# Half of the first product's tiles from seven products of quarters in blocks 2 to 5

## The chip, the cores and the metric

One Trainium2 chip, one core. The metric is the device time of one execution in microseconds (us); the kernel before has a median of 204.72 us in 3 runs.

## The reference, cut to what matters

Two stages: a recurrent attention with decay per head, and a two-layer network over its output with a leaky ramp whose slope differs by column.

```python
# q, k, v: (4, 8, 768, 64); w_in: (512, 2048); w_out: (2048, 512); alpha: (2048,)
for t in range(S):
    state = gamma * state + outer(k[:, :, t], v[:, :, t])
    y[:, :, t] = scale * q[:, :, t] @ state
x = y.transpose(0, 2, 1, 3).reshape(3072, 512)
h = x @ w_in
g = maximum(h, 0) + alpha * minimum(h, 0)
out = g @ w_out
```

## The kernel before, in words

**Blocks and units.** The 3072 tokens are 6 blocks of 512; a block is two units of 256. A unit's attention is done in chunks: GpSimd (or VectorE, early) rescales k and q by powers of the decay into `kdq` (`rescale`, L149) and casts v (`cast_v`, L162); a DMA transpose on SP's queue (`turn_dma`, L170) makes `kq`; TensorE makes state sums (`sum_mm`, L204) and scores (`score_mm`, L258); VectorE masks the scores (`masks`, L277) and adds up the state (`state`, L227: ss on VectorE, tf and tg on GpSimd or ScalarE); TensorE makes the output (`out_mm`, L289), and ScalarE evicts it, transposed, into `xT` (`take_y`, L325).

**First product** (`ffn1`, L364): gT = gate(w_inT xT) of one block, 16 tiles of 128 columns of w_in by 512 tokens. A tile is four matmuls of 512 columns into one PSUM bank. ScalarE writes hm = relu(-h) to SBUF (L389); VectorE adds (1-alpha) * hm to h from PSUM and writes f16 `gt` (L391). The tiles go in pairs f, f+8. VectorE then makes sums and differences of quarters of `gt` (`g_sums`, L351, into a tile `gs`): two of the four behind the first product, two in the second.

**Second product** (`ffn2_seven`, L433), blocks 1 to 5: out = g w_out by seven products of quarters (16 matmuls of 256 columns each) in place of eight, as `gs` and `wsum` (`w_sums`, L341) hold the sums that this takes. Their order: `gt` times w_out (1), again into `oy` (2), `gs` 1 (3), `gs` 0 (4), `gs` 2 (5), `gt` (6), `gs` 3 (7). ox and oy are PSUM banks 0 and 1. ScalarE keeps partial results (`kept`, tile `cu`), VectorE adds them to others from PSUM (`plus`, tile `os`).

**Order.** The schedule is written out by hand: each engine runs its instructions in the order in which the program emits them, and waits on semaphores for the others. `ffn1` and `ffn2_seven` are generators that yield after each matmul, and `tick(gen, m)` (L540) takes m matmuls' worth. In the loop over blocks (L703) the body emits the first product of block n with GpSimd's rescales of the units of block n+1 (the first of them held back behind the last `g_sums` by `behind`, L100), then the second product of block n with the attention of block n+1 between its pieces: after half of product 1 the state sums and scores of the first unit, after product 3 its output and the second unit's scores, after product 5 the second unit's output. Blocks 0 and 1 have a prologue of their own, written out above the loop.

**Buffers.** A tile of a tag waits until the reader of the tile that held its buffer is done. All 8 PSUM banks are addressed by number: `ps(bank, ...)`.

Of the kernel before, what the change touches and what calls it, by code (L numbers as in the profile page):

```python
# [9 lines left out]
FP = mybir.dt.float32  # L10
F16 = mybir.dt.float16
# [2 lines left out]
RELU = mybir.ActivationFunctionType.Relu  # L14
MULT = mybir.AluOpType.mult
ADD = mybir.AluOpType.add
EQUAL = mybir.AluOpType.is_equal
NOT_LESS = mybir.AluOpType.is_ge

# [2 lines left out]
def kernel(  # L22
# [117 lines left out]
    def unit(u):  # L140
        if u not in prepped:
            prepped[u] = (
                sbp.tile([128, 2, 2, H, D], F16, tag="kdq", bufs=4, name=f"kdq{u}"),
                sbp.tile([128, 4 * NP, 128], F16, tag="kq", bufs=4, name=f"kq{u}"),
                sbp.tile([128, H, 2, D], F16, tag="vx", bufs=4, name=f"vx{u}"),
            )
        return prepped[u]

# [127 lines left out]

    def masks(u, hh, parts=(0, 1)):  # L277
        for a in parts:
            m2 = sbp.tile([128, 2, 2, 128], F16, tag=f"m2{a}{hh}", bufs=2, name=f"m2{a}{hh}")
            i = nc.vector.tensor_tensor(  # L280
                out=m2,
                in0=live[u, hh][a].rearrange("p (r a i) -> p r a i", r=2, a=2),
                in1=mask.unsqueeze(2).to_broadcast([128, 2, 2, 128]),
                op=MULT,
            )
            live[u, hh][a] = m2
        return i
# [37 lines left out]
    def take_y(u, cs):  # L325
        n, ul = divmod(u, 2)
        if n not in xT:
            xT[n] = sbp.tile([128, 2, NP, U], F16, tag="xT", bufs=2, name=f"xT{n}")
# [22 lines left out]
    def g_sums(n, i, lo, hi):  # L351

        if n not in gsums:
            gsums[n] = sbp.tile([128, 4, HF, U], F16, tag="gt", bufs=2, name=f"gs{n}")
        g = gts[n].rearrange("p (k f) (j t) -> p k f j t", k=2, j=2)
        a11, a12 = g[:, 0, lo:hi, 0, :], g[:, 1, lo:hi, 0, :]
        a21, a22 = g[:, 0, lo:hi, 1, :], g[:, 1, lo:hi, 1, :]
        s1, s2, s3, s4 = (gsums[n][:, x, lo:hi, :] for x in range(4))
        o, a, b, op = (
            (s1, a21, a22, ADD), (s2, s1, a11, SUB), (s3, a11, a21, SUB), (s4, a12, s2, SUB)  # L360
        )[i]
        return nc.vector.tensor_tensor(out=o, in0=a, in1=b, op=op)  # L362

    def ffn1(n, banks, apart=0):  # L364
# [5 lines left out]
        rest = range(apart, NFT)  # L370
        if apart == 0:
            rest = [f + x for f in range(HF) for x in (0, HF)]
        turns += [(f, 1, 0, 2) for f in rest]
        for i, (f0, nf, lo, hi) in enumerate(turns):
            hps = ps(banks[i % len(banks)], "hps").rearrange("p (f t) -> p f t", f=nf)
            for f in range(nf):
                for hp in range(4):
                    nc.tensor.matmul(  # L378
                        out=hps[:, f, :].rearrange("p (u t) -> p u t", t=U),
                        lhsT=w_in_all[:, hp, 128 * (f0 + f) : 128 * (f0 + f) + 128],  # L380
                        rhs=xT[n][:, lo:hi, hp, :],
                        start=(hp == 0),
                        stop=(hp == 3),
                    )
                    if f < nf - 1 or hp < 3:
                        yield
            hm = sbp.tile([128, TB], FP, tag="hm", bufs=3, name="hm")
# [11 lines left out]
            if n > 0 and f0 in ((HF + 3, NFT - 1) if apart == 0 else (NFT - 1,)):  # L399

                lo = 0 if apart or f0 < NFT - 1 else 4
                hi = HF if f0 == NFT - 1 else 4
                g_sums(n, 0, lo, hi)
                g_sums(n, 1, lo, hi)
            yield

    def ffn2(n, banks, parts=1):
        gt = gts.pop(n)
        opss = {}
        step = NFT // parts  # L410
        for f0 in range(0, NFT, step):
            for tq in range(4):
                if f0 == 0:
                    opss[tq] = ps(banks[tq % len(banks)], "ops")
                for ft in range(f0, f0 + step):
                    nc.tensor.matmul(  # L416
                        out=opss[tq],
                        lhsT=gt[:, ft, 128 * tq : 128 * tq + 128],
                        rhs=w_out_all[:, ft, :],
                        start=(ft == 0),  # L420
                        stop=(ft == NFT - 1),
                    )
                    if ft == NFT - 1:
                        tag = ("os", "cu")[tq % 2]
                        os_sb = sbp.tile([128, d_model], FP, tag=tag, bufs=3, name=tag)
                        nc.scalar.activation(
                            out=os_sb, in_=opss[tq], func=COPY, bias=0.0, scale=1.0
                        )
                        row = TB * n + 128 * tq
                        nc.sync.dma_start(out=out[row : row + 128, :], in_=os_sb)  # L430
                    yield

    def ffn2_seven(n, x, y, z=None):  # L433
# [41 lines left out]
                        yield  # L475

        def kept(o):
            t = sbp.tile([128, 2, HM], FP, tag="cu", bufs=3, name="cu")
            for to, i in [(t, o[0])] if o[0] is not None else zip((t[:, 0, :], t[:, 1, :]), o[1]):
                nc.scalar.activation(out=to, in_=i, func=COPY, bias=0.0, scale=1.0)  # L480
            return t

        def plus(o, t, name="os"):
            so = sbp.tile([128, 2, HM], FP, tag=name, bufs=3, name=name)
            nc.vector.tensor_tensor(out=so, in0=o[0], in1=t, op=ADD)  # L485
            return so

# [188 lines left out]
    score_mm(3, 0, (4, 5))  # L676
# [106 lines left out]
```

## Time and profile before

| what | value |
|---|---|
| median of 3 runs | 204.72 us (204.43 to 205.89) |
| the profiled execution | 206.04 us |
| its span, first to last instruction | 204.3 us |
| granted TensorE clock | 1.00 in all of it |
| first products of blocks 2 to 5 start at | 85.16, 115.12, 144.84, 174.80 us |
| their length on TensorE | 13.81 us each |
| VectorE busy in that of block 3 (115.12 to 128.93) | 12.09 us |
| VectorE busy in block 3's second product (128.93 to 144.84, 15.91 us) | 12.04 us |
| ScalarE, GpSimd busy in block 3's first product | 8.96, 5.64 us |
| second product of block 5, to the end of the span | 188.61 to 204.3 us |

The engines' names: PE is TensorE, PEld its weight loads, DVE VectorE, ACT ScalarE, POOL GpSimd, SP the queue that issues most DMAs. A row of the chain or of the timeline gives start, length, engine, line, output<-inputs, shape and how many; in brackets the idle time before it and who ended it. Busy time of TensorE counts pipelined matmuls, so the spacing of matmuls is read from the chain.

### The profile page before, as it was taken

How to read it: one execution, taken by the hardware profiler on the slowest of the kernel's cores; microseconds unless marked ns; L12 is line 12 of the kernel's file. 1: busy time of each engine (PE TensorE's matmuls, PEld its weight loads, DVE VectorE, ACT ScalarE, POOL GpSimd, SP SyncE). 2: the span in 40 equal slices, each digit the busy share in tenths (PEclk: the TensorE clock that was granted, in tenths of full speed). 3: DMA queues.
4: the chain of work that ended last, by engine and by line, in shares of the span. 5: the costliest groups of instructions: out<-in, count | busy, mean ns of one | idle time of the engine just before them, and what ended most of it. 6: DMA issues, size and time to landing. Idle time of an engine off the chain costs nothing.

```text
span 204.3 us, 5491 instructions
## 1 busy us (share of the span) xinstructions
PE 195.2 (96%) x2314; PEld 128.2 (63%) x2314; DVE 157.0 (77%) x246; ACT 101.9 (50%) x169; POOL 83.3 (41%) x96
## 2 busy tenths in 40 slices
PE   7789997999999999999999999999999999999993
PEld 2457543566574788744788644788544888545882
DVE  7794985646899999189998289996489995589841
ACT  2465665236376333477353466333476254466311
POOL 2289117480269553970065960165930250000000
PEclk9999999999999999999999999999999999999999
DMA  5998999599997799399911499910570011200004
GB/s 158 337 234 134 185 253 235 157 249 173 299 346 223 153 340 304 110 258 304 284 46 41 149 250 281 300 55 22 176 166 0 3 52 57 103 0 0 21 33 154
DMA packets 64696, 33.94 MB, mean 166 GB/s; under 512 B 18064, under 2 KB 64160, under 8 KB 64672
## 3 DMA queue, kind: packets, MB, share of 16 engines
q1 hardware_dynamic: 60272, 29.37, 50.0%
q0 software_dynamic: 4224, 4.19, 13.4%
q8 instruction: 18, 0.29, 0.6%
q10 hardware_dynamic: 176, 0.03, 0.1%
q14 instruction: 6, 0.05, 0.1%
HBM read 27.30 MB, written 6.29 MB: 164 GB/s over the span
## 4 chain that ended last, share of the span: by engine, by line
PE 73%; DMA 16%; DVE 3%; POOL 2%; SPq 2%; issue 2%; ACT 0%; POOLq 0%; DVEq 0%
PE hps L378 32%; PE ox L464 16%; PE oy L464 11%; DMA qs<-in_q_dram 6%; PE ops L416 5%; DMA wout<-in_moe_w_out_dram 4%; DMA win<-in_moe_w_in_dram 4%; DMA ks<-in_k_dram 3%; PE y L313 2%; SPq L132 2%; PE sca L268 2%; PE y L298 1%; POOL tf L241 1%; PE st L215 1%; PE oz L464 1%
## 5 line engine op out<-in xcount | busy, mean ns | idle before, releaser
L378 PE MATMUL hps<-xT,win 128*128 128x512 f16 (+1 forms) x432 | 84.5, 355 | 0.1
L391 DVE SCALAR_TENSOR_TENSOR gt<-hm,oma,hps 128x512 f16<-128x512 f32 (+1 forms) x108 | 70.8, 685 | 13.6 <-ACT hm L389 8.1
L389 ACT ACTIVATE hm<-hps 128x512 f32<-128x512 f32 x96 | 57.3, 597 | 33.6 <-PE hps L378 31.4
L378 PEld LDWEIGHTS <-win 128*128 128x128 f16 x432 | 42.0, 98 | 40.3 <-DMA win<-in_moe_w_in_dram 0.8
L464 PEld LDWEIGHTS <-gs 128*128 128x128 f16 x320 | 31.0, 98 | 3.9
L241 POOL TENSOR_TENSOR tf<-ss,tab 128x256 f32<-128x256 f32 x16 | 12.2, 765 | 35.7 <-DVE ss L240 34.7
L464 PEld LDWEIGHTS <-gt 128*128 128x128 f16 x240 | 22.8, 98 | 4.8
L152 POOL TENSOR_TENSOR kdq<-ks,tab 128x1024 f16<-128x1024 f32 (+1 forms) x10 | 17.3, 1729 | 18.8 <-issue 9.8
L480 ACT ACTIVATE cu<-ox 128x512 f32<-128x512 f32 (+1 forms) x18 | 9.5, 526 | 29.9 <-PE ox L464 29.7
L256 POOL CAST tg<-tf 64x256 f16<-64x256 f32 x29 | 14.2, 488 | 20.0 <-DVE tf L237 18.6
L485 DVE TENSOR_TENSOR os<-oy,cu 128x512 f32<-128x512 f32 x14 | 9.6, 689 | 16.2 <-PE oy L464 13.7
L152 POOL TENSOR_TENSOR kdq<-qs,tab 128x1024 f16<-128x1024 f32 (+1 forms) x13 | 20.7, 1594 | 1.9 <-DMA qs<-in_q_dram 1.9
L280 DVE TENSOR_TENSOR m<-sca,mi 128x512 f16<-128x512 f32 x24 | 16.4, 684 | 4.2 <-PE scb L268 4.2
L464 PE MATMUL ox<-wsum,gs 128*128 128x256 f16 x160 | 19.1, 273 | 0.0
L331 ACT ACTIVATE xT<-y 128x512 f16<-128x512 f32 x24 | 16.2, 741 | 5.6 <-PE y L313 5.5
L280 DVE TENSOR_TENSOR m<-scb,mi 128x512 f16<-128x512 f32 x24 | 16.3, 681 | 0.0
L416 PE MATMUL ops<-wout,gt 128*128 128x512 f16 x64 | 15.2, 380 | 0.2 <-DMA wout<-in_moe_w_out_dram 0.2
L168 POOL CAST vx<-vs 128x1024 f16<-128x1024 f32 (+1 forms) x13 | 12.5, 973 | 5.6 <-DMA vs<-in_v_dram 5.6
L362 DVE TENSOR_TENSOR gs<-gt 128x1024 f16<-128x1024 f16 (+1 forms) x14 | 12.9, 922 | 0.3
L254 ACT ACTIVATE tg<-tf 64x256 f16<-64x256 f32 x11 | 4.6, 414 | 15.6 <-POOL tf L241 10.4
L188 ACT ACTIVATE kq<-trb 128x1024 f16<-128x1024 f16 x8 | 8.2, 1024 | 6.7 <-PE trb L182 6.5
L464 PE MATMUL ox<-wout,gt 128*128 128x256 f16 x80 | 10.4, 274 | 0.0
(50 smaller groups left out, 175.1 us busy)
## 6 DMA issues: line engine op xcount, KB each, us to landing
out_dram<-os SPq DMA_DIRECT2D x21, 256.0 KB, 2.3
vs<-in_v_dram SPq DMA_DIRECT2D x10, 512.0 KB, 6.4
ks<-in_k_dram SPq DMA_DIRECT2D x8, 512.0 KB, 4.6
qs<-in_q_dram SPq DMA_DIRECT2D x8, 512.0 KB, 5.5
ks<-in_k_dram SPq DMA_DIRECT2D x8, 256.0 KB, 4.7
qs<-in_q_dram SPq DMA_DIRECT2D x8, 256.0 KB, 4.8
win<-in_moe_w_in_dram POOLq DMA_DIRECT2D x4, 512.0 KB, 8.0
wout<-in_moe_w_out_dram POOLq DMA_DIRECT2D x4, 512.0 KB, 8.5
```

The source lines that it names most:

```text
L152: return eng.tensor_tensor(out=kdq[:, t, :, h0:h1, :].rearrange("p r h d -> p h r d"), in0=staged[u]["kq"[t]][:, h0:h1, :].rearrange("p h ...
L168: eng.tensor_copy(out=o, in_=i)
L241: eng.tensor_tensor(out=t, in0=ss, in1=dec, op=MULT)
L256: nc.gpsimd.tensor_copy(out=o, in_=i)
L280: i = nc.vector.tensor_tensor(out=m2, in0=live[u, hh][a].rearrange("p (r a i) -> p r a i", r=2, a=2), in1=mask.unsqueeze(2).to_broadcast([ ...
L331: nc.scalar.activation(out=xT[n][:, ul, :, 128 * c : 128 * c + 128].rearrange("k a (p r) -> k a r p", r=2), in_=ys[c].rearrange("k (a r p) ...
L362: return nc.vector.tensor_tensor(out=o, in0=a, in1=b, op=op)
L378: nc.tensor.matmul(out=hps[:, f, :].rearrange("p (u t) -> p u t", t=U), lhsT=w_in_all[:, hp, 128 * (f0 + f) : 128 * (f0 + f) + 128], rhs=x ...
L389: nc.scalar.activation(out=hm, in_=hps, func=RELU, bias=0.0, scale=-1.0)
L391: nc.vector.scalar_tensor_tensor(out=gt[:, f0 + f, U * lo : U * hi], in0=hm[:, f, :], scalar=oma_sb[:, f0 + f : f0 + f + 1], in1=hps[:, f, :],
L416: nc.tensor.matmul(out=opss[tq], lhsT=gt[:, ft, 128 * tq : 128 * tq + 128], rhs=w_out_all[:, ft, :], start=(ft == 0), stop=(ft == NFT - 1),)
L464: nc.tensor.matmul(out=o[1][m], lhsT=lhs(f, m), rhs=rhs(f), start=(first and f == 0 and (m == 0 or o[0] is None)), stop=(f == HF - 1), ski ...
```

## The change

In the first product of blocks 2 to 5, the tiles 0 to 3 and 8 to 11 are made as two groups (g = 0, 1) of two-by-two quarters: rows are the tile halves (i = 0: tiles 2g, 2g+1; i = 1: tiles 8+2g, 9+2g), columns the two units j of the block, and the contraction is halved too. Seven products of four 256-column matmuls give the four quarters c11, c21, c12, c22 of a group. This takes sums of quarters of w_in (`wi_sums`, once, on VectorE in the prologue) and of `xT` (`x_sums`, per block, on VectorE). The other eight tiles (`one`) are made as before and lie between the groups. ScalarE keeps c1, u2 and u3, VectorE adds them to PSUM (`plus`: c11, c22, c12, in SBUF as f32), and c21 comes from PSUM. c11 and c22 are gated on GpSimd (`gate_pool`), c21 and c12 by ScalarE's relu and VectorE's gate, by quarters. To make room, `kdq`, `kq`, `vx` go from 4 to 3 buffers, `m2` and `xT` from 2 to 1; `hm` goes from 3 to 5, `cu` from 3 to 4. `ffn1` stays for blocks 0 and 1.

```diff
+    amo_sb = sbp.tile([128, 128], FP, tag="amo", name="amo")[:, 0:NFT]
+    SEV = 4
+    visum = sbp.tile([128, 4, 2, 128 * SEV], F16, tag="visum", name="visum")
...
+    def wi_sums(x):
+        a11, a12 = wi_quarter(0, 0, 0, SEV), wi_quarter(0, 1, 0, SEV)
+        a21, a22 = wi_quarter(1, 0, 0, SEV), wi_quarter(1, 1, 0, SEV)
+        s1, s2, s3, s4 = (visum[:, y] for y in range(4))
+        o, a, b, op = (
+            (s1, a21, a22, ADD), (s2, s1, a11, SUB), (s3, a11, a21, SUB), (s4, a12, s2, SUB)
+        )[x]
+        nc.vector.tensor_tensor(out=o, in0=a, in1=b, op=op)
...
+    def x_sums(n):
+        t = sbp.tile([128, 4, 2, U], F16, tag="xsum", name=f"xsum{n}")
+        xsum[n] = t
+        (b11, b21), (b12, b22) = (
+            [xT[n][:, j, 2 * k : 2 * k + 2, :] for k in range(2)] for j in range(2)
+        )
+        t1, t2, t3, t4 = (t[:, y] for y in range(4))
+        for o, a, b in ((t1, b12, b11), (t2, b22, t1), (t3, b22, b12), (t4, b21, t2)):
+            nc.vector.tensor_tensor(out=o, in0=a, in1=b, op=SUB)
...
+        def gate_pool(i, g, h, j):
+            f = HF * h + 2 * g
+            hm = sbp.tile([128, TB], FP, tag="hm", bufs=5, name="hm")
+            for x in range(2):
+                c = slice(U * x, U * x + U)
+                nc.gpsimd.tensor_scalar(
+                    out=hm[:, c],
+                    in0=i[:, c],
+                    scalar1=0.0,
+                    scalar2=amo_sb[:, f + x : f + x + 1],
+                    op0=MIN,
+                    op1=MULT,
+                )
+            nc.gpsimd.tensor_tensor(
+                out=gt[:, f : f + 2, U * j : U * j + U],
+                in0=hm.rearrange("p (f t) -> p f t", f=2),
+                in1=i.rearrange("p (f t) -> p f t", f=2),
+                op=ADD,
+            )
...
+        def product(p, g, o, first):
+            for x in range(2):
+                w = lhs(p, 2 * g + x)
+                for h in range(2):
+                    nc.tensor.matmul(
+                        out=o[:, U * x : U * x + U],
+                        lhsT=w[h],
+                        rhs=rhs[p][:, h, :],
...
+        def plus(o, t):
+            so = sbp.tile([128, TB], FP, tag="os", bufs=3, name="os")
+            nc.vector.tensor_tensor(out=so, in0=o, in1=t, op=ADD)
+            return so
...
+        yield from one(SEV, 7)
+        yield from one(HF + SEV, 2)
+        yield from one(SEV + 1, 3)
+        for g in range(2):
+            X[g] = ps((4, 6)[g], "hx")
+            yield from product(1, g, X[g], True)
+            c1[g] = kept(X[g])
+            yield
+        for g in range(2):
+            Y[g] = ps((5, 1)[g], "hy")
+            yield from product(2, g, Y[g], True)
+            c11[g] = plus(Y[g], c1[g])
+            yield
+        yield from one(HF + SEV + 1, 0)
+        for g in range(2):
+            yield from product(6, g, X[g], False)
+            u2[g] = kept(X[g])
+            gate_pool(c11[g], g, 0, 0)
+            yield
+        for g in range(2):
+            yield from product(5, g, Y[g], True)
+            yield
+        yield from one(SEV + 2, 7)
+        for g in range(2):
+            yield from product(7, g, X[g], False)
+            u3[g] = kept(X[g])
+            c22[g] = plus(Y[g], u3[g])
+            gate_pool(c22[g], g, 1, 1)
+            yield
+        yield from one(HF + SEV + 2, 2)
+        for g in range(2):
+            yield from product(4, g, X[g], False)
+            gate_by(X[g], relu(X[g]), parts(g, 1, 0))
+            yield
+        yield from one(SEV + 3, 3)
+        for g in range(2):
+            yield from product(3, g, Y[g], False)
+            c12[g] = plus(Y[g], u2[g])
+            yield
+        yield from one(HF + SEV + 3, 7)
+        for g in range(2):
+            gate_by(c12[g], relu(c12[g]), parts(g, 0, 1))
+        for lo, hi in ((SEV, HF), (0, SEV)):
+            g_sums(n, 0, lo, hi)
+            g_sums(n, 1, lo, hi)
...
+    V.tensor_scalar(out=amo_sb, in0=oma_sb, scalar1=-1.0, scalar2=None, op0=MULT)
     w_sums(0, 0, HF)
     tick(gen, 9)
     out_mm(2, (4, 5))
     tick(gen, 10)
-    tick(half, 24)
+    tick(half, 16)
+    wi_sums(0)
+    wi_sums(1)
+    tick(half, 8)
+    wi_sums(2)
     turn_pe(3, 0, 6)
     tick(half, 8)
+    wi_sums(3)
...
-            gen = ffn1(n, (7, 2, 3, 1, 0, 6, 5, 4, 7, 1, 0, 4, 5, 6, 7, 1))
+            gen = ffn1_mixed(n)
...
             out_mm(u0 + 1, (4, 5))
+            x_sums(n + 1)
```

More of the change, by code (lines that the diff above doesn't have):

```diff
@@ L16 @@
 ADD = mybir.AluOpType.add
+MIN = mybir.AluOpType.min
 EQUAL = mybir.AluOpType.is_equal
@@ new lines, with ffn1_mixed, one, relu @@
+    xsum = {}
+    def x_sums(n):
[7 more added lines that the diff above has]
+            nc.vector.tensor_tensor(out=o, in0=a, in1=b, op=SUB)
+    def ffn1_mixed(n):
+        gt = sbp.tile([128, NFT, TB], F16, tag="gt", bufs=2, name=f"gt{n}")
+        gts[n] = gt
+        b = [[xT[n][:, j, 2 * k : 2 * k + 2, :] for j in range(2)] for k in range(2)]
+        xs = [xsum[n][:, y] for y in range(4)]
+        def one(f, bank):
+            hps = ps(bank, "hps")
+            for hp in range(4):
+                nc.tensor.matmul(
+                    out=hps.rearrange("p (u t) -> p u t", t=U),
+                    lhsT=w_in_all[:, hp, 128 * f : 128 * f + 128],
+                    rhs=xT[n][:, :, hp, :],
+                    start=(hp == 0),
+                    stop=(hp == 3),
+                )
+                if hp < 3:
+                    yield
+            gate_by(hps, relu(hps), [(f, 0, 2, 0)])
+            yield
+        def relu(i):
+            hm = sbp.tile([128, TB], FP, tag="hm", bufs=5, name="hm")
+            nc.scalar.activation(out=hm, in_=i, func=RELU, bias=0.0, scale=-1.0)
+            return hm
+        def gate_by(i, hm, parts):
+            for f, lo, hi, at in parts:
+                c = slice(at, at + U * (hi - lo))
+                nc.vector.scalar_tensor_tensor(
+                    out=gt[:, f, U * lo : U * hi],
+                    in0=hm[:, c],
+                    scalar=oma_sb[:, f : f + 1],
+                    in1=i[:, c],
+                    op0=MULT,
+                    op1=ADD,
+                )
+        def gate_pool(i, g, h, j):
+            f = HF * h + 2 * g
+            hm = sbp.tile([128, TB], FP, tag="hm", bufs=5, name="hm")
+            for x in range(2):
[7 more added lines that the diff above has]
+                    op1=MULT,
+                )
+            nc.gpsimd.tensor_tensor(
[3 more added lines that the diff above has]
+                op=ADD,
+            )
+        def lhs(p, f):
+            if p in (1, 2, 4):
+                i, k = ((0, 0), (0, 1), (1, 1))[(1, 2, 4).index(p)]
+                w = wi_quarter(i, k, f, f + 1)
+            else:
+                w = visum[:, {3: 3, 5: 0, 6: 1, 7: 2}[p], :, 128 * f : 128 * f + 128]
+            return [w[:, h, :] for h in range(2)]
+        rhs = {1: b[0][0], 2: b[1][0], 3: b[1][1], 4: xs[3], 5: xs[0], 6: xs[1], 7: xs[2]}
+        def product(p, g, o, first):
+            for x in range(2):
+                w = lhs(p, 2 * g + x)
+                for h in range(2):
+                    nc.tensor.matmul(
+                        out=o[:, U * x : U * x + U],
+                        lhsT=w[h],
+                        rhs=rhs[p][:, h, :],
+                        start=(first and x == 0 and h == 0),
+                        stop=(h == 1),
+                        skip_group_check=True,
+                    )
+                    if x == 0 or h == 0:
+                        yield
+        def kept(o):
+            t = sbp.tile([128, TB], FP, tag="cu", bufs=4, name="cu")
+            nc.scalar.activation(out=t, in_=o, func=COPY, bias=0.0, scale=1.0)
+            return t
+        def plus(o, t):
+            so = sbp.tile([128, TB], FP, tag="os", bufs=3, name="os")
+            nc.vector.tensor_tensor(out=so, in0=o, in1=t, op=ADD)
+            return so
+        def parts(g, i, j):
+            return [(HF * i + 2 * g + x, j, j + 1, U * x) for x in range(2)]
+        X, Y, c1, u2, u3, c11, c22, c12 = ({} for _ in range(8))
+        yield from one(SEV, 7)
[26 more added lines that the diff above has]
+            gate_pool(c22[g], g, 1, 1)
+            yield
+        yield from one(HF + SEV + 2, 2)
+        for g in range(2):
+            yield from product(4, g, X[g], False)
+            gate_by(X[g], relu(X[g]), parts(g, 1, 0))
+            yield
+        yield from one(SEV + 3, 3)
+        for g in range(2):
+            yield from product(3, g, Y[g], False)
+            c12[g] = plus(Y[g], u2[g])
+            yield
+        yield from one(HF + SEV + 3, 7)
[4 more added lines that the diff above has]
+            g_sums(n, 1, lo, hi)
@@ L369, in ffn1 @@
         turns = [(f, 2, ul, ul + 1) for ul in range(2) for f in range(0, apart, 2)]
[L370 to L373, printed above, removed]
+        turns += [(f, 1, 0, 2) for f in range(apart, NFT)]
         for i, (f0, nf, lo, hi) in enumerate(turns):
@@ L398, in ffn1 @@
                 )
[L399 to L404, printed above, removed]
+            if n > 0 and f0 == NFT - 1:
+                g_sums(n, 0, 0, HF)
+                g_sums(n, 1, 0, HF)
             yield
@@ L483, in plus @@
         def plus(o, t, name="os"):
-            so = sbp.tile([128, 2, HM], FP, tag=name, bufs=3, name=name)
+            so = sbp.tile([128, 2, HM], FP, tag=name, bufs=4 if name == "cu" else 3, name=name)
             nc.vector.tensor_tensor(out=so, in0=o[0], in1=t, op=ADD)
```

20 lines of the change are left out of this document (11 added, 9 removed).

## The prediction

> **What bounds the kernel now.** I read the page's busy shares first, then the chain of waits in order of time, then VectorE's timeline behind one first product, then GpSimd's rows beside it. Block 3 stands for blocks 2 to 4. From the page and from the chain (start, us, what):
>
> ```profile
> PE 195.2 (96%) x2314; PEld 128.2 (63%) x2314; DVE 157.0 (77%) x246; ACT 101.9 (50%) x169; POOL 83.3 (41%) x96
> ```
> ```profile
> 115.12 13.81 PE hps L378 x64
> 128.93 0.91 PE ox L464 x8
> ...
> 131.89 1.75 PE oy L464 x16
> 133.64 1.75 PE ox L464 x16
> ```
>
> TensorE runs without a gap. A first product is 64 matmuls of 512 columns in 13.81 us (215.8 ns each); in the second product 16 of 256 columns take 1.75 us (109.3 ns each). So fewer columns are less time, if nobody else is late. Who is near to late is VectorE:
>
> ```profile
> 130.38 0.69 DVE L362 TENSOR_TENSOR gs<-gt 128x1024 f16<-128x1024 f16 x1
> 131.11 0.69 DVE L362 TENSOR_TENSOR gs<-gs,gt 128x1024 f16<-128x1024 f16 x1
> 131.72 0.41 DVE L240 TENSOR_TENSOR ss<-tf,st 128x256 f32<-128x256 f32 x1
> ...
> 134.18 0.68 DVE L280 TENSOR_TENSOR m<-scb,mi 128x512 f16<-128x512 f32 x1
> ```
>
> The sums of gated tiles end at 131.80, 2.9 us behind TensorE's last first-product matmul, and the product that reads them (133.64) has only 1.8 us in hand. Behind the sums in VectorE's queue stand the state's sums and the masks of the next block's unit, to 134.86; TensorE needs the last mask at about 136. The whole queue, from the gates to 140.45, has no gap. In block 1 the same queue was later, and TensorE waited 0.43 us for a mask.
>
> Third, VectorE and GpSimd get in each other's way when both read operands from SBUF (VectorE, then GpSimd):
>
> ```profile
> 55.19 0.68 DVE L349 TENSOR_TENSOR wsum<-wout,wsum 128x1024 f16<-128x1024 f16 x1
> 55.79 1.10 DVE L349 TENSOR_TENSOR wsum<-wout 128x1024 f16<-128x1024 f16 x1
> ```
> ```profile
> 55.42 0.93 POOL L241 TENSOR_TENSOR tf<-ss,tab 128x256 f32<-128x256 f32 x1 [2.14 <-DVE ss L240]
> ```
>
> GpSimd's tf takes 0.61 alone; here it waits for the first w_sum and then holds up the second, 1.10 for 0.68. They take turns, though VectorE's two were back to back. Gates, which read one operand from PSUM, leave GpSimd's rescale at its usual 1.90.
>
> **TensorE: less.** Before, 64 x 215.8 ns = 13.81. After, eight whole tiles, 32 x 215.8 = 6.91, and seven products of four matmuls in two groups, 56 x 109.3 = 6.12: 13.03. That is -0.78 a block, -3.1 for blocks 2 to 5. The 24 more weight loads take 98 ns each, under the 109 of a matmul.
>
> **VectorE: more, and later.** Spacing in its queue: a 512 gate 0.685 (eight in 5.54); a 256 gate 0.42 (six in 2.62); a plus 0.60 (134.78 to 135.38); four half sums 2.76 (two such pairs). Before: 16 x 0.685 + 2.76 = 13.7. After: 8 x 0.685 + 8 x 0.42 + 6 x 0.60 + 2.76 = 15.2, so +1.5 in a stage that is 0.78 shorter. The four 256 gates of c12 read both operands from SBUF, which no gate here does: 0.33 (spacing of ss, 256) to 0.69 each; I keep 0.42.
>
> x_sums adds four 128x512 f16 operations: 0.42 each, on the line through 0.69 (1024) and 1.22 (2048). They lie where VectorE was idle (the 3.07 us before the last plus), but read two SBUF operands just while GpSimd rescales the next units. With F the first matmul of block 2, the first rescale runs from F-3.74 (81.42), xT is ready at F-2.23 (82.93), and in turns the four end at F-1.88 + 4 x 0.42 + 1.86 + 1.00 + 1.86 = F+4.5. Bounds: 1.7 us with no turns lost (end F-0.5), 6.4 with the turns. I take the turns, as each such overlap in the trace shows them.
>
> The Trainium skill, "SBUF — State Buffer", section "SBUF: two separate sides", says the shared port pair is an exclusive lock that the first holds for its whole instruction. The rows above agree for a 0.61 us instruction; none shows it for one of 1.9.
>
> **What is queued behind x_sums.** All times from F, the first matmul of the stage.
> - The last plus of the old second product is next, to F+5.1. It frees PSUM bank 1, which is Y[1]: TensorE is at product 2 of the second group by F+3.9 and waits 1.2.
> - Gates of tiles 4, 12 and 5 to F+7.15, then c11 of both groups to F+7.75 and F+8.35. Product 5 overwrites Y and waits for them, TensorE's second wait.
> - Gate 13 to 9.05. Tile 6 ends on TensorE at F+9.65, and a gate follows 0.7 behind its tile (as 116.65 behind 115.98): 10.35 to 11.0. VectorE idles 1.3 before it.
> - c22 to 12.2, gate 14 to 12.9, four quarter gates of c21 to 14.55, gate 7 to 15.25, c12 to 16.45, gate 15 to 17.1, four gates of c12 to 18.8, the sums to F+21.6. TensorE's part ends at F+14.9.
>
> The same list without the turns ends at F+19.8 and TensorE at F+13.0: VectorE then idles from 6.6 to 8.5, while products 6 and 5 give it nothing to gate, and is never ahead again.
>
> The rescales that waited their turn end 1.7 later, and with them the transposes and loads that follow on SP's queue; their data are first read in the second product, 7 us behind the last rescale, so I cost that at nothing (if that cover failed, up to 1.7 a block).
>
> **What is late next.** Product 3 would start 4.7 after the stage's end (133.64 less 128.93), F+19.6; it waits 2.0 for the sums (0.5 of it already at the scores into bank 7, freed by gate 15). From there the next block was 11.2 to 11.4 away. Now the last mask comes 3.1 to 3.7 after the sums (134.86 less 131.80; block 1 76.02 less 72.32), and TensorE is there after 1.75 + 0.45 + 0.28 = 2.5: 0.6 to 1.2 more, with scores behind the state's sum 1.0 on average. Block: 21.6 + 11.3 + 1.0 = 33.9 to 34.1, for 29.7 to 30.0: +4.2, three times, 12.6. Block 5 has no rescales to take turns with and no attention in its second product; product 3 is due at 13.03 + 3.53 = 16.56 and waits for 19.8: 3.3 less 0.78, +2.5.
>
> **GpSimd.** A gate_pool is two tensor_scalar of 256, not in the trace: 0.40 (the 64x256 cast) to 0.61 (tf) each; and an add of 512, 1.03 (the 512 rescale) to 1.10. So 1.8 to 2.3; I take 1.95, by the cast, which also reads one operand. It starts after rescales and casts, F+7.4, and c11: F+7.8, 9.7, 11.7, 13.7, 15.6. Its readers: c12 through the three os buffers, hm of tiles 7 and 15 through the five hm buffers, the last two sums. Tile 15's relu must start by F+15.8. At 1.95 it is covered, by 0.2; at 2.3 it ends 17.0, and the block loses 1.1.
>
> **The rest.** wi_sums (4 x 0.60) and amo_sb (0.17) go into VectorE's gaps of 1.31, 0.53 and 1.52 between 43 and 51.2 us; masks then start some 0.3 later: +0.2, between 0 and 2.6 if all of it showed. One buffer less of kdq, kq, vx, m2 and xT costs nothing: each new writer stands behind a product that TensorE has finished. Uncovered, an m2 would wait for one out_mm, 1.0 us a block.
>
> **Sum.** 12.6 + 2.5 + 0.2 = +15.3. The profiled execution took 206.04 (span 204.3 and 1.74 around it), 1.3 over the median 204.72. On its own time that is 221.3, on the median 220.0.
>
> **Rivals.**
> - No turns lost at the port. Sums by F+19.8, but GpSimd, free at F+7.4, now holds hm of tiles 7 and 15 (13.1 and 15.0), +0.9: 3 x 3.25 + 2.5 + 0.2 = +12.5, 217. Against it: every overlap in the trace.
> - GpSimd's gates dearer. At 2.3 each, +1.1 in three blocks, 223.5; at 3.2 tile 15's relu would wait to F+20.6, +4.8 in three blocks and +3.1 in the last, 237. For it: only 0.2 us in hand and an operation without a row.
> - TensorE's clock falls in block 5's 3.3 us wait. No gap in the trace is that long while it works, and the granted clock was 1.00 in every stretch. Each product of 16 run at half clock costs 1.75; two give 223.5. The Trainium skill, "TensorE: Matmul & The Clock Gate", "Part 1: The HAM clock gate", has the clock halved after an idle window of about 3.4 us, close to this wait.
> - Faster: VectorE's lateness stays hidden. Its place is product 3 of the second product: if the sums end within 4.7 us of TensorE's last first-product matmul, only the columns count, -3.1: 201.6. Now they end 2.9 behind; it would need 2.0 us less than I count, in each block. Against it: already with no port loss the sums come 6.8 behind.
> - No change: half of that lateness is absorbed, and the waits just pay for the columns, about 0.8 a block.
>
> **Chances.** Forecast 0.57, no turns 0.15, dearer gates 0.17, clock 0.03, faster 0.04, no change 0.04. So faster by over 1% 0.04, within 1% (about what a measurement can tell) 0.04, slower 0.92. The range runs from below the no-turns case with cheap SBUF gates (4 x 0.09 less in four blocks and hm waits gone, 213) to gates at about 2.6 each (228); beyond lie the two small cases and the far end of the dear gates.
>
> **What would show it.** Right: in the changed profile hps and products fill 13 us of TensorE per block; x_sums last over 1 us each on average and alternate with rescales; the last gs ends 6 to 7 us behind the stage; TensorE waits for DVE gs at product 3 (2 us in blocks 2 to 4, 3 in block 5), for masks after it, and for a plus at bank 1. Wrong: x_sums at 0.42 each (no turns), tensor_scalar on GpSimd over 0.6 (dearer gates), product 3 directly behind product 2 (faster), a granted clock under 1 in block 5.

## The result, and the profile after

The changed kernel takes 246.41 us (median of 4 runs, 244.72 to 248.44) where the kernel before takes 204.74 on the same chip (4 runs): 1.200 times as long, interval 1.191 to 1.208. (Here and below, a ratio leaves out a single run in a slower state of the chip, here the 248.44.) The prediction had the direction; 220.0 was 26 short, and the range ended at 228. The profiled execution took 245.96 with a span of 243.8.

The page of the changed kernel: busy times, the granted clock in 40 slices, the chain's shares by engine, and the two groups that GpSimd's gates make.

```profile
PE 206.9 (85%) x2410; PEld 144.0 (59%) x2410; DVE 184.5 (76%) x291; ACT 103.0 (42%) x177; POOL 142.4 (58%) x144
...
PEclk9999999999999999958999965999995999997679
...
POOL 36%; PE 26%; DVE 16%; DMA 9%; issue 8%; ACT 2%; SPq 1%; POOLq 1%; DVEq 0%
...
L445 POOL TENSOR_SCALAR hm<-os,amo 128x256 f32<-128x256 f32 x32 | 36.2, 1139 | 13.6 <-DVE os L494 13.6
...
L453 POOL TENSOR_TENSOR gt<-hm,os 128x512 f16<-128x512 f32 x16 | 20.2, 1264 | 1.3
```

The chain's shares before were:

```profile
PE 73%; DMA 16%; DVE 3%; POOL 2%; SPq 2%; issue 2%; ACT 0%; POOLq 0%; DVEq 0%
```

GpSimd, which carried 2% of the chain, carries 36%. A tensor_scalar of 256 columns takes 1.139 us, an add of 512 takes 1.264: a gate_pool is 3.5 us of work, 3.59 from one to the next, where the prediction had 1.95. And the granted clock, 1.00 in every slice before, falls in each block, in block 5 twice (it is 0.62 from 220 to 222 us and 0.50 from 228 to 234).

The start of each block's first product, F, is the ruler for the rest. It lies at 84.15, 124.55, 163.85 and 203.74, and the end at 243.8: blocks of 40.40, 39.30, 39.89 and 40.06, against 29.97, 29.72, 29.95 and 29.67 before. Every block loses 9.6 to 10.5, block 5 as much as the others. Here is the chain of waits through block 2 (F = 84.15), and the end of block 5:

```profile
102.19 2.25 POOL hm L445 x2
...
104.51 1.27 POOL gt L453
...
105.81 0.61 ACT hm L424
...
106.44 2.33 DVE gt L430 x5
108.77 0.61 DVE gs L368
...
110.73 0.69 DVE gs L368
...
228.85 3.60 PE ox L641 x16
232.45 2.64 PE oy L641 x16
235.09 1.75 PE ox L641 x16
```

GpSimd's four gates run from 91.39 to 105.77 without a gap. The moment the last lets go of its hm buffer, ScalarE writes tile 15's relu into it (105.81), VectorE gates tile 15 and the last quarters, and only then come the sums, which end at 111.42. That is F+27.3, 13.0 us behind TensorE's last first-product matmul (98.44); it was 2.9 behind before. In block 5 the products 3 and 4 take 3.60 and 2.64, where the next takes 1.75.

The waits of the changed kernel say the same from the waiting side (who, for whom: us in total, times, longest):

```profile
ACT hm L424 <- POOL gt L453: 23.9, 9, 3.0
...
PE ox L641 <- DVE gt L430: 16.2, 4, 4.3
...
PE scb L274 <- DVE gt L430: 5.4, 3, 2.1
```

ScalarE's in-order queue waits for GpSimd, VectorE for ScalarE, and TensorE for VectorE: for tile 7 in product 1 (up to 4.3 us) and for the bank of tile 15 at the scores. VectorE's timeline in block 2 shows the port turns that were forecast, and the new idle time that was not:

```profile
82.12 0.73 DVE L395 TENSOR_TENSOR xsum<-xT 128x512 f16<-128x512 f16 x1 [1.06 <-ACT xT L337]
82.88 2.01 DVE L395 TENSOR_TENSOR xsum<-xT,xsum 128x512 f16<-128x512 f16 x1
84.81 1.25 DVE L395 TENSOR_TENSOR xsum<-xT 128x512 f16<-128x512 f16 x1
85.99 2.12 DVE L395 TENSOR_TENSOR xsum<-xT,xsum 128x512 f16<-128x512 f16 x1
...
106.44 0.75 DVE L430 SCALAR_TENSOR_TENSOR gt<-hm,oma,hps 128x512 f16<-128x512 f32 x1 [1.64 <-ACT hm L424]
...
110.73 0.69 DVE L368 TENSOR_TENSOR gs<-gs,gt 128x1024 f16<-128x1024 f16 x1
```

The x_sums end at F+3.9 (forecast F+4.5), the last plus of the old product follows, and TensorE's part ends at F+14.3 (forecast F+14.9). The account holds up to there; it fails behind GpSimd's gates.

### The profile page after: what moved, and what is told of

It reads as the page before. It is cut to its first block, busy times and chain, and to the rows that moved or that the text cites. A ratio compares the mean times of both kernels' runs of the same rounds, so it can differ in the third digit from the quotient of the medians.

```text
span 243.8 us, 5806 instructions
## 1 busy us (share of the span) xinstructions
PE 206.9 (85%) x2410; PEld 144.0 (59%) x2410; DVE 184.5 (76%) x291; ACT 103.0 (42%) x177; POOL 142.4 (58%) x144
## 4 chain that ended last, share of the span: by engine, by line
POOL 36%; PE 26%; DVE 16%; DMA 9%; issue 8%; ACT 2%; SPq 1%; POOLq 1%; DVEq 0%
POOL hm L445 14%; PE hps L558 10%; POOL gt L453 8%; POOL kdq L158 8%; DVE gs L368 5%; PE ox L641 4%; DVE gt L430 4%; PE ops L593 4%; DVE m L286 3%; DMA wout<-in_moe_w_out_dram 3%; POOL vx L174 3%; DMA vs<-in_v_dram 3%; PE oy L641 3%; DMA ks<-in_k_dram 2%; POOL tf L247 2%
## 5 line engine op out<-in xcount | busy, mean ns | idle before, releaser
L445 POOL TENSOR_SCALAR hm<-os,amo 128x256 f32<-128x256 f32 x32 | 36.2, 1139 | 13.6 <-DVE os L494 13.6
L641 PEld LDWEIGHTS <-gt 128*128 128x128 f16 x240 | 25.5, 111 | 25.7 <-DVE gt L430 17.8
L430 DVE SCALAR_TENSOR_TENSOR gt<-hm,oma,hps 128x512 f16<-128x512 f32 x32 | 23.3, 741 | 22.1 <-ACT hm L424 21.9
L424 ACT ACTIVATE hm<-hps 128x512 f32<-128x512 f32 x32 | 19.1, 597 | 44.5 <-PE hps L410 22.2
L410 PE MATMUL hps<-xT,win 128*128 128x512 f16 x128 | 31.5, 379 | 0.0
L571 DVE SCALAR_TENSOR_TENSOR gt<-hm,oma,hps 128x256 f16<-128x256 f32 (+1 forms) x44 | 25.2, 600 | 4.7 <-ACT hm L569 2.8
L558 PE MATMUL hps<-xT,win 128*128 128x256 f16 (+1 forms) x176 | 28.4, 321 | 0.0
L641 PE MATMUL ox<-wout,gt 128*128 128x256 f16 x80 | 14.6, 335 | 16.2 <-DVE gt L430 16.2
L558 PEld LDWEIGHTS <-win 128*128 128x128 f16 x176 | 17.1, 98 | 10.6
L569 ACT ACTIVATE hm<-hps 128x512 f32<-128x512 f32 x32 | 19.1, 597 | 9.3 <-PE hps L558 9.3
L262 POOL CAST tg<-tf 64x256 f16<-64x256 f32 x29 | 14.1, 486 | 14.6 <-DVE tf L243 13.3
L453 POOL TENSOR_TENSOR gt<-hm,os 128x512 f16<-128x512 f32 x16 | 20.2, 1264 | 1.3
L410 PEld LDWEIGHTS <-win 128*128 128x128 f16 x128 | 12.5, 98 | 10.0
```

Of the source, the lines that this page charges most:

```text
L410: nc.tensor.matmul(out=hps.rearrange("p (u t) -> p u t", t=U), lhsT=w_in_all[:, hp, 128 * f : 128 * f + 128], rhs=xT[n][:, :, hp, :], star ...
L424: nc.scalar.activation(out=hm, in_=i, func=RELU, bias=0.0, scale=-1.0)
L430: nc.vector.scalar_tensor_tensor(out=gt[:, f, U * lo : U * hi], in0=hm[:, c], scalar=oma_sb[:, f : f + 1], in1=i[:, c], op0=MULT, op1=ADD,)
L445: nc.gpsimd.tensor_scalar(out=hm[:, c], in0=i[:, c], scalar1=0.0, scalar2=amo_sb[:, f + x : f + x + 1], op0=MIN, op1=MULT,)
L453: nc.gpsimd.tensor_tensor(out=gt[:, f : f + 2, U * j : U * j + U], in0=hm.rearrange("p (f t) -> p f t", f=2), in1=i.rearrange("p (f t) -> ...
L558: nc.tensor.matmul(out=hps[:, f, :].rearrange("p (u t) -> p u t", t=U), lhsT=w_in_all[:, hp, 128 * (f0 + f) : 128 * (f0 + f) + 128], rhs=x ...
```

## The experiments

Two theories to start with. **Queue of dear gates**: tensor_scalar on GpSimd costs twice what was bounded, and all that the change loses beyond the forecast hangs on the hm buffers that it holds; the rest of the forecast is right. **Port and lateness**: VectorE's own late start (the turns of x_sums) is the larger part, and GpSimd's gates fill time in which VectorE is late anyway. Times are one run each beside the kernel before on the same chip, unless an interval is given.

**The price by itself (m_forms).** The kernel before, with forms of GpSimd instructions in block 5, where GpSimd is idle. They work on scratch tiles, and nothing reads them.

```diff
+    def forms():
...
+            G.tensor_scalar(out=o[:, 0:256], in0=a[:, 0:256], scalar1=0.0, scalar2=col, op0=MIN, op1=MULT)
+            G.tensor_scalar(out=o[:, 0:256], in0=a[:, 0:256], scalar1=0.0, scalar2=0.7, op0=MIN, op1=MULT)
+            G.tensor_scalar(out=o[:, 0:256], in0=a[:, 0:256], scalar1=col, scalar2=None, op0=MULT)
+            G.tensor_scalar(out=o[:, 0:256], in0=a[:, 0:256], scalar1=0.7, scalar2=None, op0=MULT)
+            G.tensor_scalar(out=o[:, 0:512], in0=a[:, 0:512], scalar1=0.0, scalar2=col, op0=MIN, op1=MULT)
...
+            G.tensor_copy(out=o[:, 0:256], in_=a[:, 0:256])
...
+            else:
+                forms()
```

> The kernel before, with nine forms of GpSimd instruction three times over in block 5, where GpSimd was idle; their outputs are read by nobody. The changed profile has the tensor_scalar of 256 columns with minimum, multiply and a slope per partition at 1.14 us. If the per-partition operand is the cost, the form with two constants is 0.4 to 0.6 and the single multiply by a column stays near 1.1. If the second operation is the cost, both single multiplies are 0.4 to 0.6 and the two-constant form stays near 1.1. If it is a fixed cost of the instruction, 512 columns take under 1.5 and all tensor_scalar forms are near 1.1; if it is a cost per element, 512 columns take about 2.1. Casts of 256 near 0.40, adds of 256 at 0.61, adds of 512 to f16 at 1.03 to 1.27. The time stays at 204.7 within 1.

204.57 us for 205.28. GpSimd's timeline of this kernel (start, us, line; fa the input, oma the operand per partition):

```profile
171.58 2.00 POOL L715 TENSOR_SCALAR fo<-fa,oma 128x512 f32<-128x512 f32 x1
...
177.06 1.15 POOL L711 TENSOR_SCALAR fo<-fa,oma 128x256 f32<-128x256 f32 x1
178.30 1.07 POOL L712 TENSOR_SCALAR fo<-fa 128x256 f32<-128x256 f32 x1
179.47 0.93 POOL L713 TENSOR_SCALAR fo<-fa,oma 128x256 f32<-128x256 f32 x1
180.48 0.85 POOL L714 TENSOR_SCALAR fo<-fa 128x256 f32<-128x256 f32 x1
...
184.92 0.39 POOL L717 COPY fo<-fa 128x256 f32<-128x256 f32 x1
...
186.09 1.27 POOL L719 TENSOR_TENSOR fh<-fa 128x512 f16<-128x512 f32 x1
```

None of the single causes carries it. The operand per partition costs 0.08, the second operation 0.21; the leanest tensor_scalar (0.85) is still twice the copy (0.39). From 256 to 512 columns the price goes from 1.14 to 2.00, 3.4 ns a column. It is the instruction, not a form of it, it is paid by the column more than by the call, and one call of 512 columns would save only 0.28.

**The ramp taken out (e_cast).** Gate_pool becomes one copy of 512 into `gt`, at the same places and behind the same c11 and c22. It is one instruction of 0.61 us, and it takes no hm buffer any more, so this run takes away the price and the hold on the ring together.

```diff
-            for x in range(2):
...
-                nc.gpsimd.tensor_scalar(
...
-            nc.gpsimd.tensor_tensor(
+            nc.gpsimd.tensor_copy(
                 out=gt[:, f : f + 2, U * j : U * j + U],
...
+                in_=i.rearrange("p (f t) -> p f t", f=2),
```

> The changed kernel; GpSimd copies c11 and c22 into gt (one cast of 512 each) and leaves out their ramp. Theory: the price of GpSimd's gates alone is what the forecast had wrong, and the rest of its sum stands: 220 us (216 to 224), the last gs near F+21.6, waits of TensorE of about 2 us before product 3, granted clock back near 1.0. Rival: the mixed order itself is late (VectorE and ScalarE behind the products, the clock falling in the waits), and GpSimd's length is covered by that: 235 or more.

219.86 us for 205.28. The span is 218.2, 25.6 less than with the ramp. What TensorE waits for (us in total, times, longest) is now the list that the prediction gave:

```profile
PE ox L628 <- DVE gs L368: 6.3, 4, 2.9
PE y L319 <- DVE m L286: 2.6, 4, 1.0
...
PE hy L463 <- DVE os L649: 1.5, 3, 0.6
```

The sums at product 3, the masks behind it, the plus that frees bank 1. Blocks: 33.94, 32.94, 33.45, 33.73. So the rest of the forecast stands, and the ramp on GpSimd, with the buffers that it holds, is the missing 26. One term of the sum is there that the forecast had put among the rivals, in TensorE's timeline of block 5:

```profile
204.09 2.84 PE L628 MATMUL ox<-wsum,gs 128*128 128x256 f16 x16 [2.94 <-DVE gs L368]
206.72 2.70 PE L628 MATMUL oy<-wsum,gs 128*128 128x256 f16 x16
209.26 1.91 PE L628 MATMUL ox<-wsum,gs 128*128 128x256 f16 x16
```

Start to start, products 3 and 4 take 5.17 where the next two take 3.49: 1.7 us to a clock that fell during a wait of 2.94.

**The turns taken out (e_cast_held).** As e_cast, and GpSimd's first rescale waits for the last x_sum, so that they never meet.

```diff
-            x_sums(n + 1)
+            gate = x_sums(n + 1)
```

> As the run with casts, the ramp of c11 and c22 left out, and the first rescale of the next units is held back behind x_sums instead of behind the last g_sums, so that the four x_sums meet no rescale. Theory: the turns at the port cost 1.8 us of VectorE's queue in blocks 2 to 4 and it all shows: x_sums at 0.42 to 0.73 each, last gs near F+19.8, and 5 to 6 us less than the run with casts, about 214. Rival: VectorE's idle time before gate 6 takes up the turns, and the times are within 1.5 us of each other. Second rival: the rescales, 2 us later now, hold up the casts and so the sums: slower than the run with casts.

216.3 us, 3.6 less than e_cast. VectorE's timeline: x_sums back to back at 0.42, and the wait that remained in block 3.

```profile
82.05 0.42 DVE L395 TENSOR_TENSOR xsum<-xT 128x512 f16<-128x512 f16 x1 [1.06 <-ACT xT L337]
82.50 0.42 DVE L395 TENSOR_TENSOR xsum<-xT,xsum 128x512 f16<-128x512 f16 x1
...
125.39 0.75 DVE L431 SCALAR_TENSOR_TENSOR gt<-hm,oma,hps 128x512 f16<-128x512 f32 x1 [1.86 <-ACT hm L425]
```

The turns are real, but only part of them was on the path: each of blocks 2 to 4 gains 1.1 to 1.3, not 1.7 to 2.0. VectorE, early, idles 1.86 before a gate whose tile TensorE has not made yet.

**The same edit with the dear gates (e_held).** The changed kernel, with that one line and nothing else.

> The changed kernel, GpSimd's gates as they are, with the first rescale held back behind x_sums. With GpSimd's cheap casts this edit took 3.6 us away. Theory: in the changed kernel GpSimd's own queue (rescales, then four gates of 3.58) sets each block, so the same edit now costs: the gates start some 2.6 us later in blocks 2 to 4, 250 to 255 us. Rival: the waits of VectorE at the port are what is late, and the edit helps here too: 241 to 244.

251.92 us for 204.7: 5.5 more than the changed kernel. GpSimd's timeline in block 2 (the changed kernel's first rescale starts at 80.67, its last gate at 104.51):

```profile
83.94 1.90 POOL L158 TENSOR_TENSOR kdq<-ks,tab 128x1024 f16<-128x1024 f32 x1 [6.73 <-DVE xsum L395]
...
106.47 1.26 POOL L454 TENSOR_TENSOR gt<-hm,os 128x512 f16<-128x512 f32 x1
```

The edit that gains 3.6 when GpSimd's gates are cheap costs 5.5 when they are dear. GpSimd starts 3.3 later, gets 1.3 of it back (its rescales no longer take turns, and c11 is there when they end), and its last gate ends 2.0 later; the block is 42.31 for 40.40. This tells the two theories apart: GpSimd's queue sets the block, and a faster VectorE is worth nothing.

**Buffers apart (e_hm).** Two buffers of their own for GpSimd's hm, three for ScalarE's; five in all, as in the change.

```diff
-            hm = sbp.tile([128, TB], FP, tag="hm", bufs=5, name="hm")
+            hm = sbp.tile([128, TB], FP, tag="hm", bufs=3, name="hm")
...
-            hm = sbp.tile([128, TB], FP, tag="hm", bufs=5, name="hm")
+            hm = sbp.tile([128, TB], FP, tag="hq", bufs=2, name="hq")
```

> The changed kernel, with buffers of their own (two) for hm of GpSimd's gates, and three for all other hm, so that the relus of tiles 7 and 15 wait for no buffer of GpSimd's. Theory: they wait for those buffers alone now; then the last sums wait for GpSimd's last gate itself (F+21.6) and end near F+23 instead of F+27.3: 4 us less a block, 228 to 233 us. Rival: the tiles would be as late through the three os buffers of c12 or through P1's operands, and the time stays within 3 us of the changed kernel's 246.

236.05 us for 204.7, 10.4 under the changed kernel's median; the blocks are 37.89, 36.87, 37.39 and 37.0, 2.4 to 3.1 less each. Less than was expected, and the timelines of VectorE and, in the last row, of GpSimd show why:

```profile
103.26 0.69 DVE L494 TENSOR_TENSOR os<-hy,cu 128x512 f32<-128x512 f32 x1 [2.75 <-POOL gt L453]
...
104.52 2.75 DVE L430 SCALAR_TENSOR_TENSOR gt<-hm,oma,os 128x256 f16<-128x256 f32 x4
...
105.56 1.44 POOL L453 TENSOR_TENSOR gt<-hq,os 128x512 f16<-128x512 f32 x1
```

The wait moved to the next ring of buffers that GpSimd holds: c12 of the second group needs the third `os`, which GpSimd's gate still reads. Its four quarter gates then meet GpSimd's last add at the port: they take 2.75 for the 1.67 of the changed kernel, and 1.48 of that is the last gate alone, which ends after the add. So the hm ring is 10.4 of what the gates cost; the rest stays while GpSimd's gates are this long. The first theory had the cost right and the buffers too narrow.

**The ramp on ScalarE (e_act).** GpSimd keeps the add; ScalarE makes relu((alpha - 1) h) with a scale per partition, which is the (1 - alpha) relu(-h) that GpSimd made.

```diff
-                nc.gpsimd.tensor_scalar(
+                nc.scalar.activation(
                     out=hm[:, c],
...
+                    func=RELU,
+                    bias=0.0,
+                    scale=amo_sb[:, f + x : f + x + 1],
```

> The changed kernel, nothing left out: the ramp of c11 and c22 is made by ScalarE (relu with a slope per partition, four of 256 columns a group) and GpSimd only adds (one of 512). Theory: GpSimd at 1.03 to 1.27 a quarter is off the path, ScalarE has 3 us more per block of which about half shows: 222 to 226 us. Rival: ScalarE, which now waits for c11 and c22 in order ahead of the relus of tiles 6 and 14, holds up VectorE as GpSimd did: 232 or more.

234.26 us for 205.28; blocks of 37.17, 36.09, 36.68 and 38.6. The waits:

```profile
PE hx L475 <- ACT cu L488: 5.8, 4, 1.7
...
ACT hm L445 <- DVE os L493: 7.0, 8, 0.9
```

ScalarE takes its work in order, so a ramp that waits for VectorE's c11 and c22 stands ahead of the copies (`cu`) that TensorE waits for. That is the longest of TensorE's waits, not all of them: it also waits 5.1 us for gates in product 1 and 4.1 for sums. Giving an engine cheap work that comes late costs what is queued behind it.

**The clock kept up (e_spin).** The changed kernel with constant matmuls, which nothing reads, in block 5's two long waits.

```diff
-            tick(gen, 33)
+            tick(gen, 7)
+            keep(16, 6)
+            tick(gen, 25)
+            keep(14, 6)
+            tick(gen, 1)
```

> The changed kernel, with 16 and 14 matmuls of a constant tile in block 5's second product, in TensorE's waits before tile 7 and before product 3; their output is read by nobody. Theory: the granted clock falls to a half in waits over some 3 us, and in block 5 products 3 and 4 lose 2.7 us by it (3.60 and 2.64 for 1.75 each): with TensorE busy they take 1.75 each, and block 5, from its first matmul to the end, takes 37.2 to 37.7 instead of 39.9. Rival: those products are slow because their operands come late, and the block stays at 39.9 or longer.

244.38 us for 204.7. The whole time is no measure here, since block 2 began 1.1 later than in the profile of the changed kernel, with the same code ahead of it. Block 5 is: 37.56 us, where it was 40.06. TensorE's timeline:

```profile
226.71 3.19 PE L97 MATMUL kps<-spin 128*128 128x512 f16 x14
229.96 1.92 PE L641 MATMUL ox<-wsum,gs 128*128 128x256 f16 x16
231.72 1.91 PE L641 MATMUL oy<-wsum,gs 128*128 128x256 f16 x16
233.47 1.91 PE L641 MATMUL ox<-wsum,gs 128*128 128x256 f16 x16
```

Product 3 starts 25.1 after the block's start, as in the changed kernel, so its operands are no earlier. Products 3 and 4 start 1.76 and 1.75 apart again, and the granted clock is 1.00 from 228 to 233. The fallen clock was 2.5 us of block 5.

**Half of the idea, rebuilt (e_one, e_two).** One group of quarters in place of two (tiles 6, 7, 14, 15; 0.40 us of columns less a block). ScalarE makes every slope with a scale per partition, so that the gates are plain adds, on GpSimd for c11, c22 and c12; the first rescale is held as in e_cast_held. e_two gives GpSimd's hm its own ring, takes the f of the second product in the order in which gates come, and makes c12's ramp one tile later.

```diff
-    SEV = 4
...
+    S0, SEV = 6, 8
...
+            hm = slopes(hps, ((f, 0, TB),))
+            nc.vector.tensor_tensor(out=gt[:, f, :], in0=hm, in1=hps, op=ADD)
...
+        yield from one(8, 2)
+        gate_quarter(G, c11, 0, 0)
...
+            gate = x_sums(n + 1)
```

> A version after what the runs showed: one group instead of two (tiles 6, 7, 14, 15 by seven products), every slope on ScalarE (relu with a slope per partition), plain adds on VectorE for whole tiles and c21 and on GpSimd for c11, c22 and c12, no tensor_scalar on GpSimd, rescales held back behind x_sums, tiles in an order that keeps VectorE fed. TensorE saves 0.39 a block, 1.6 in all. Theory: VectorE's stage is 12.4 us of work (13.7 before), ends about 3.3 behind TensorE (2.9 before), and nearly all of the 1.6 is had: 203.2 to 204.2 against 204.7. Rival: ScalarE, which now has 13 us in a stage of 13.4, falls behind and the masks come late: 205 to 209.

e_one: 208.78 us (208.38 to 211.82), ratio to before 1.0185 (1.0147 to 1.0223). TensorE's timeline at product 1 of block 2 shows where it loses: it needs tiles 4 and 5 before VectorE has them.

```profile
99.27 0.28 PE L617 MATMUL ox<-wout,gt 128*128 128x256 f16 x1 [0.80 <-DVE gt L421]
99.87 0.50 PE L617 MATMUL ox<-wout,gt 128*128 128x256 f16 x3 [0.31 <-DVE gt L421]
```

```diff
+            own = (("hq", 3) if eng is nc.gpsimd else ("hm", 4))
+            hm = slopes(i, ((f, 0, U), (f + 1, U, TB)), *own)
...
+                    f = (0, 1, 2, 3, 6, 7, 4, 5)[k]
```

> The one-group version again, with the two waits that its trace showed taken away: buffers of their own for the slopes that GpSimd adds (ScalarE waited 1.0 a block for them), and product 1 of the second product takes tiles 4 and 5 last (TensorE waited 0.8 and 0.3 a block for their gates). Theory: those 2 us a block were all that it lost, blocks of 29.4 to 29.8, and it beats the kernel before: 203 to 204.5. Rival: VectorE is simply as late as its work is long, the wait moves to the scores or the masks, 206 to 209.

e_two: 205.54 us (204.75 to 206.44), ratio 1.0011 (0.9985 to 1.0038), no difference from before. The first product does take 13.42 us for 13.82, in every block. It comes back at once: in block 3 the first eight matmuls of product 1 take 1.32 (127.86 to 129.18) for 0.91 before, and product 1 of block 5 takes 2.30 (187.39 to 189.69) for 1.78 before, since it now has to stop for the last gates:

```profile
187.39 0.93 PE L619 MATMUL ox<-wout,gt 128*128 128x256 f16 x7
188.50 1.16 PE L619 MATMUL ox<-wout,gt 128*128 128x256 f16 x9 [0.18 <-DVE gt L421]
189.69 1.91 PE L619 MATMUL oy<-wout,gt 128*128 128x256 f16 x16
```

The four blocks are 30.31, 29.66, 29.87 and 29.93, together 119.8 for 119.3 before. That is the prediction's "no change" rival, at half the size.

**The control (e_ctl).** The kernel before with only the other gate: slopes on ScalarE, plain adds on VectorE.

```diff
+                nc.scalar.activation(
+                    out=hm, in_=hps, func=RELU, bias=0.0, scale=amo_sb[:, f0 : f0 + 1]
+                )
+                nc.vector.tensor_tensor(out=gt[:, f0, :], in0=hm[:, 0, :], in1=hps[:, 0, :], op=ADD)
```

> The kernel before with nothing of the seven products, only the cheaper gate of the one-group version in blocks 2 to 5: slope on ScalarE, plain add on VectorE (0.60 for 0.685 of its queue). Theory: TensorE had no gap there, so nothing is gained: 204.7 within 0.5; what the one-group version gains or loses is then its own. Rival: VectorE's earlier end shows in the masks: 203.5 or less.

204.8 us (204.33 to 208.73), ratio 0.9999 (0.9976 to 1.0022). The other gate alone moves nothing, so what e_two gains and loses is not the gate's. (Its order and its buffers differ too, and were not run apart.) No version here beats the kernel before.

## Why the prediction was right and wrong

**The step that failed: the price of GpSimd's tensor_scalar.** The prediction said "two tensor_scalar of 256, not in the trace: 0.40 (the 64x256 cast) to 0.61 (tf) each; and an add of 512, 1.03 (the 512 rescale) to 1.10". Measured: 1.14 and 1.26. Both lie outside their bounds, the first by a factor of nearly two. So a gate was sized at 1.95 and takes 3.59, and the cover of 0.2 us that the prediction gave the hm ring was not there. The rows were near in size but of other instructions, and the choice within them went by the number of operands ("by the cast, which also reads one operand"). m_forms shows that this is not what sets the price: with one operand each, the copy of 256 columns takes 0.39 and the tensor_scalar 0.85 to 1.14. The Trainium skill, "GPSIMD Engine Reference", section "4.1 Engine selection", says that work with one input runs on GpSimd at roughly the line rate; the copy may agree with that, and these tensor_scalars, at 3.4 ns a column, do not.

**The rival that came true.** "GpSimd's gates dearer" had the place, the mechanism and the point from which it decides: tile 15's relu waits for GpSimd through the five hm buffers. Its own rule, carried to the measured 3.59 per gate, gives 4.8 + 4 x 0.39 = 6.4 a block over the forecast. Measured, the changed kernel less e_cast: 6.46, 6.36 and 6.44 in blocks 2 to 4. (Two smaller misses cancel there: the gates began at F+7.2 rather than F+7.8, and product 2, at half clock, let product 3 start only at 112.11, 0.7 behind the sums.) In block 5 the rule gives 3.1 + 1.6 = 4.7 and the difference is 6.3; 0.8 of that is the costlier fall of the clock (2.5 for 1.7), and the rest is open. The rival had a chance of 0.17 and a far end at 237; the range stopped at gates of 2.6. With 0.2 us in hand and no row for the instruction, that was too narrow.

**The rest of the sum was about right, and not for each of its terms.** e_cast has gates that are cheaper still than the forecast's (0.61 for 1.95, and no hm buffer), which by the forecast's list is no gain, as its gates were covered; a gate of 1.95 was not run. It takes 14.6 over before; the forecast was 15.3. By block the forecast was +4.2 three times and +2.5. Measured: +4.0, +3.2, +3.5, and in block 5 +4.1, of which 1.7 is the fallen clock, so +2.4 without it. Then 0.85 comes off ahead of block 2. Since e_spin began block 2 a whole 1.1 us later than the changed kernel with the same code up to there, that 0.85 lies within the spread of the prologue and is no gain; wi_sums show no cost against it.

**Turns at the port.** Right in kind: x_sums and rescales alternate ahead of blocks 2 to 4, with two of the four x_sums at 2.0 to 2.1 for 0.42 and rescales at 2.08 for 1.90; ahead of block 5, where no rescale runs, all four take 0.42 to 0.43. The Trainium skill, "SBUF — State Buffer", section "SBUF: two separate sides", has the pair as an exclusive lock; the trace now shows it for instructions of 1.9 us too, but m_forms does not show it for tensor_scalar (last section). The turns' price was a little too high: e_cast_held says 1.1 to 1.3 a block, and the prediction's no-turns list 1.8 at the sums, with VectorE's idle time ahead of later tiles as the difference.

**The clock.** It was a rival of block 5 alone, at 0.03. With the dear gates' longer waits it fell in all four blocks, and in e_cast in block 5 as well. The Trainium skill, "TensorE: Matmul & The Clock Gate", "Part 1: The HAM clock gate", has the clock halved after an idle window of about 3.4 us; the runs agree in kind, but 2.94 us of waiting was enough in e_cast and e_cast_held. So the 3.3 us wait that the prediction itself forecast should have had this priced into its main sum.

**The saving.** Fewer columns came as counted (13.42 for 13.82 with one group), and never reached the end of the block in any version. The reason given, that VectorE is near to late and the first product's end is where it is late, is what e_two shows.

## What to carry to other kernels

An instruction that no trace shows has no price from rows of like size: copies, adds and tensor_scalars of the same 256 columns took 0.39, 0.73 and 1.14 us on one engine, so take the range wide, or measure it in a place where the engine is idle. When work goes to a slow engine, follow the buffers that it holds; the wait shows up on an engine that has nothing to do with it (here ScalarE, through the hm ring), and splitting the ring moves it to the next one. Columns taken from TensorE are worth something only if the engine that gates the last of them is not due at that very moment.

## What the runs showed of the hardware

- GpSimd's tensor_scalar: 1.14 us for 256 columns of 128 partitions, 2.00 for 512; a constant in place of the operand per partition 1.07, one operation 0.93 or 0.85, f16 output again 1.14. Beside VectorE's work on two SBUF operands they took up to 1.84 (256) and 3.45 (512).
- Turns at the port held between x_sums and rescales: an x_sum of 0.42 takes 2.0 when a rescale of 1.9 is running. They did not hold for tensor_scalar. In m_forms one of 512 columns took 3.45 for 2.00, while two sums of VectorE ran past it, one behind the other, at their usual 1.2:

```profile
191.35 1.24 DVE L363 TENSOR_TENSOR gs<-gt 128x2048 f16<-128x2048 f16 x1
192.51 1.21 DVE L363 TENSOR_TENSOR gs<-gt,gs 128x2048 f16<-128x2048 f16 x1
```
```profile
192.06 3.45 POOL L715 TENSOR_SCALAR fo<-fa,oma 128x512 f32<-128x512 f32 x1
```

- TensorE's clock fell to 0.50 after waits of 2.94 to 4.27 us, and stayed there for 3 us (205 to 208 in e_cast) to 10 us (142 to 152 in the changed kernel). It cost 1.7 us in block 5 of e_cast and 2.5 in that of the changed kernel. The waits of e_cast's blocks 2 to 4, 1.1 us each on average at product 3, left it at 1.00. The length of one wait does not decide it: in e_act the clock was 0.50 from 104 to 106 in block 2, behind waits of 1.26 and 0.64 with state sums and scores between them, and 1.00 in block 4 behind waits of 1.26 and 0.67.
